# First batch of a Fourier and spatial-gating kernel: even transform summed as the fold goes, V by four products, W cast one piece ahead, four more W tiles ahead

## The chip, the cores and the metric

The kernel runs on one core of a Trainium2 chip. The metric is the device time of one execution in microseconds; where several executions are given, the median with the lowest and highest. TensorE is PE in the profile (its weight loads PEld), VectorE DVE, ScalarE ACT, GpSimd POOL, SyncE SP. All runs told here were in the fast state (mean granted clock, which is the TensorE clock in the profile as a share of full speed, 0.982 to 0.998 for the profiled ones), and all gave the right result. A DMA share is the mean busy share of the core's 16 DMA engines.

## The reference

```python
# x (8, 3072, 256), w_in (256, 1024), w_spatial W (3072, 3072), w_out (512, 256)
X = np.fft.fft(x, axis=1)
X = np.fft.fft(X, axis=2)
x = X.real.astype(np.float32)
h = np.maximum(x @ w_in, 0.0)
u, v = h[..., :512], h[..., 512:]
mu, var = mean(v), mean((v - mu) ** 2)           # over the last axis (cut)
v_n = (v - mu) / np.sqrt(var + 1e-06)
v_s = np.einsum('ts,bsd->btd', W, v_n) + b_spatial[None, :, None]
return ((u * v_s) @ w_out).astype(np.float32)
```

## The kernel before

Eight batches pass one after the other. For each, DVE folds x into even and odd sums, PE multiplies these with sine and cosine tables (the transform, four residues, even and odd halves in `eo`; a few rows are handled apart by a small product, the special columns or "specials", whose result is added when the transform leaves PSUM), then come the products with the folded `w_in` (V and U), then the big product with W, the spatial product. W must be transposed once, during the first batch, in 96 pieces of 128 x 768: load, cast to bf16, six transposes on PE, a copy out of PSUM into a W tile of four pieces, and a store of the finished tile for the later batches. There are 24 such tiles per batch (counted from 0 here), each used by four spatial groups of six products; after the fourth tile of every output chunk its output projection follows, so the first projection runs within tile 4. The tables, the first transform, the first V and the transposition of W all belong to the first 316 us.

A piece is cast when it is turned, so its transposes always wait for its own cast:

```python
def turn_w(wt, first=False):
    ...
    if first:
        nc.scalar.copy(out=wb, in_=src)              # cast on ACT, during the start
    else:
        nc.gpsimd.tensor_copy(out=wb, in_=src)       # cast on Pool, later
    load_w()
    for kk in range(GK):                             # six transposes on PE
        nc.tensor.transpose(pt[:, kk, :], wb[:, 128 * kk:128 * kk + 128], ident)
    ...                                              # copy to wt on DVE or ACT
    if r == 3:
        nc.scalar.dma_start(out=wtd[c][g], in_=wt)   # store of the finished tile
```

V is made for rows in mirrored pairs, with three products: their sum `pv`, and `pd`, twice the odd product. The mirrored row is `pv - pd`. It takes a copy on ACT and a subtraction on DVE:

```python
def v_pair(i, eo, pr):
    for kt in range(2):                              # pv = even + odd
        nc.tensor.matmul(pv, lhsT=eo[:, kt, sl], rhs=weo[:, kt, DH:], ...)
    nc.tensor.matmul(pd, lhsT=eo[:, 1, sl], rhs=wo2[:, DH:], ...)   # 2 x odd
    nc.scalar.activation(out=r[0], in_=pv, func=AF.Relu)
    nc.scalar.copy(out=m_, in_=pd)
def v_minus(...):
    nc.vector.tensor_tensor(out=r[1], in0=pv, in1=pd, op=ALU.subtract)
    ...                                              # statistics of r[0]
def v_relu(...):
    nc.scalar.activation(out=r[1], in_=r[1], func=AF.Relu)
# then: statistics of r[1] (DVE), root (ACT), reciprocal (DVE), norm (one half on ACT, one on DVE)
```

The start, in the order of issue: tables; three W pieces; per part of x an even fold, a piece, an odd fold, a piece; the special columns; then `dct_even` and `dct_odd` with a piece after each of the four residues; then V, in small steps among pieces. The pieces are capped at the four tiles that the spatial loop is ahead (`AHEAD = 4`).

## Time and profile before

| | before |
|---|---|
| time, 3 runs | 1420.38 us (1416.41 to 1420.64) |
| span of the profile, mean granted clock | 1418.0 us, 0.984 |
| first V product / sixth V pair normalised / twelfth | 69.05 / 98.76 / 133.67 |
| first output projection (tile 4) / second (tile 8) / fifth (tile 20) | 155.10 / 191.28 / 297.64 |

The span in 40 slices of 35.5 us each, a digit being the busy share in tenths (kernel before). Nearly all that PE loses lies in the first six slices, and its slow clock lies there too:

```profile
PE   0557989999999999999999999999999999999998
PEclk9968999999999999999999999999999999999999
DMA  7854888887444563345443563445434553444441
```

One V pair in the timeline of the kernel before (start, duration, engine, instruction, and in brackets the idle time of its engine before it with what ended that). DVE and ACT wait for each other in turn: ACT's norm for DVE's rs, DVE's statistics for ACT's Relu, which stands behind that norm. The round takes 94.53 - 90.31 = 4.22 us, though neither engine is full.

```profile
90.31 0.81 ACT L507 ACTIVATE v_t<-r,rs 128x512 bf16<-128x512 f32 x1 [1.62 <-DVE rs L505]
91.03 0.61 ACT L484 ACTIVATE r<-r 128x512 f32<-128x512 f32 x1
...
91.68 0.69 DVE L494 BATCH_NORM_STATS2 stt<-r 128x6 f32<-128x512 f32 x1 [1.01 <-ACT r L484]
...
94.53 0.81 ACT L507 ACTIVATE v_t<-r,rs 128x512 bf16<-128x512 f32 x1 [1.62 <-DVE rs L505]
```

### The profile page before, as it was taken

The page shows a single profiled execution, that of the slowest core. Times are in us where ns is not written, and L with a number is a line of the kernel's source. Part 1 is how long each engine was busy: PE and PEld are TensorE (multiplying, and loading weights), DVE is VectorE, ACT ScalarE, POOL GpSimd, SP SyncE. Part 2 cuts the span into 40 slices and gives each one's busy share as a digit, 9 for nine tenths or more (in the row PEclk, how much of TensorE's full clock was granted, in tenths as well). Part 3 has the DMA queues.
Part 4 walks back from the last instruction along what each step waited for, and adds up shares of the span by engine and source line. Part 5 has one row for each costly group of instructions (what it writes and reads, how often), then busy time and mean ns, then how long its engine had stood idle before and what let it go on. Part 6 is the DMA issues. An engine that isn't in the chain of part 4 may idle for free.

```text
span 1418.0 us, 18127 instructions
## 1 busy us (share of the span) xinstructions
PE 1327.9 (94%) x6955; PEld 651.9 (46%) x6955; DVE 860.4 (61%) x1715; ACT 515.9 (36%) x888; POOL 126.1 (9%) x167
## 2 busy tenths in 40 slices
PE   0557989999999999999999999999999999999998
PEld 0313545554444444444444444444444444444444
DVE  7465856676566755587376755587376755662323
ACT  4565235642245304441245314531345214541110
POOL 9112433440000000000000000000000000000000
PEclk9968999999999999999999999999999999999999
DMA  7854888887444563345443563445434553444441
GB/s 228 285 175 144 316 327 255 298 316 258 176 134 148 165 231 111 134 149 200 159 146 134 182 219 104 135 150 200 176 127 139 181 186 116 144 151 143 148 160 52
DMA packets 105255, 255.29 MB, mean 180 GB/s; under 512 B 17584, under 2 KB 64336, under 8 KB 105168
## 3 DMA queue, kind: packets, MB, share of 16 engines
q1 hardware_dynamic: 65840, 196.66, 41.9%
q10 hardware_dynamic: 29824, 44.05, 8.6%
q0 software_dynamic: 9504, 13.42, 3.0%
q8 instruction: 54, 0.88, 0.3%
q14 instruction: 33, 0.27, 0.1%
HBM read 210.80 MB, written 56.62 MB: 189 GB/s over the span
## 4 chain that ended last, share of the span: by engine, by line
PE 84%; DMA 3%; DVE 3%; ACT 1%; ACTq 0%; issue 0%; POOL 0%; SPq 0%; DVEq 0%; POOLq 0%
PE pw L543 66%; PE po L559 6%; PE pu L521 3%; PE pv L466 3%; PE pt L183 2%; PE pe L428 1%; PE pud L523 1%; PE pd L468 1%; DMA wr<-in_moe_w_spatial_dram 1%; DMA xt<-xr 1%; DVE tm L549 1%; DVE gt L550 1%; DVE xt L349 0%; DMA xt<-in_x_dram 0%; PE p L488 0%
## 5 line engine op out<-in xcount | busy, mean ns | idle before, releaser
L543 PE MATMUL pw<-wt,v_t 128*128 128x512 bf16 x4608 | 1054.5, 381 | 10.6 <-ACT v_t L507 10.5
L543 PEld LDWEIGHTS <-v_t 128*128 128x128 bf16 x4608 | 447.0, 98 | 530.2 <-issue 13.4
L563 ACT COPY ot<-po 128x512 f32<-128x512 f32 x96 | 56.3, 586 | 383.8 <-PE po L559 376.6
L549 DVE TENSOR_TENSOR tm<-pw,bbc 128x512 f32<-128x512 f32 x192 | 131.4, 684 | 95.0 <-PE pw L543 85.8
L507 ACT ACTIVATE v_t<-r,rs 128x512 bf16<-128x512 f32 x96 | 78.5, 817 | 108.7 <-DVE rs L505 102.3
L183 PE MATMUL pt<-ident,wb 128*128 128x128 bf16 x576 | 52.6, 233 | 52.1 <-ACT wb L177 45.7
L559 PE MATMUL po<-wob,gt 128*128 128x256 bf16 x768 | 99.7, 273 | 1.7 <-DVE gt L550 1.7
L526 ACT ACTIVATE up<-pu 128x512 bf16<-128x512 f32 x96 | 57.3, 597 | 110.8 <-PE pu L521 75.0
L179 POOL CAST wb<-wr 128x768 bf16<-128x768 f32 x87 | 75.8, 873 | 173.0 <-PE pt L183 136.7
L559 PEld LDWEIGHTS <-gt 128*128 128x128 bf16 x768 | 74.7, 98 | 29.3 <-DVE gt L550 2.2
L494 DVE BATCH_NORM_STATS2 stt<-r 128x6 f32<-128x512 f32 x96 | 65.3, 681 | 28.7 <-ACT r L484 28.2
L183 PEld LDWEIGHTS <-wb 128*128 128x128 bf16 x576 | 42.6, 104 | 77.9 <-ACT wb L177 48.4
L499 ACT ACTIVATE rs<-mv,epst 128x2 f32<-128x2 f32 x96 | 28.5, 297 | 120.1 <-DVE mv L495 112.9
L484 ACT ACTIVATE r<-r 128x512 f32<-128x512 f32 x96 | 60.2, 627 | 29.5 <-DVE r L478 27.6
L466 PE MATMUL pv<-weo,eo_t 128*128 128x512 bf16 x192 | 60.2, 397 | 10.8 <-ACT wt L188 3.4
L550 DVE SCALAR_TENSOR_TENSOR gt<-up,tm 128x512 bf16<-128x512 bf16 x96 | 67.5, 704 | 3.3
L550 DVE SCALAR_TENSOR_TENSOR gt<-um,tm 128x512 bf16<-128x512 bf16 x96 | 66.9, 696 | 3.3
L470 ACT ACTIVATE r<-pv 128x512 f32<-128x512 f32 x96 | 56.3, 586 | 33.0 <-PE pv L466 30.3
L188 ACT COPY wt<-pt 128x768 bf16<-128x768 bf16 x53 | 42.2, 796 | 65.5 <-PE pt L183 65.4
L479 DVE BATCH_NORM_STATS2 stt<-r 128x6 f32<-128x512 f32 x96 | 65.6, 684 | 0.0
L521 PE MATMUL pu<-eo_t,weo 128*128 128x512 bf16 x192 | 57.1, 379 | 0.0
L509 DVE TENSOR_SCALAR v_t<-r,mv,rs 128x512 bf16<-128x512 f32 x96 | 53.0, 553 | 0.0
(607 smaller groups left out, 971.6 us busy)
## 6 DMA issues: line engine op xcount, KB each, us to landing
wt<-wtd SPq DMA_DIRECT2D x168, 768.0 KB, 4.3
wr<-in_moe_w_spatial_dram SPq DMA_DIRECT2D x69, 384.0 KB, 4.5
out_dram<-ot ACTq DMA_DIRECT2D x88, 256.0 KB, 3.7
wtd<-wt ACTq DMA_DIRECT2D x24, 768.0 KB, 5.8
xr<-in_x_dram POOLq DMA_DIRECT2D x32, 384.0 KB, 11.3
xt<-in_x_dram SPq DMA_DIRECT2D x21, 512.0 KB, 4.2
xt<-xr SPq DMA_DIRECT2D x21, 512.0 KB, 6.5
wr<-in_moe_w_spatial_dram SPq DMA_DIRECT2D x23, 383.5 KB, 8.0
```

What stands on the lines that cost most here:

```text
L179: nc.gpsimd.tensor_copy(out=wb, in_=src)
L183: nc.tensor.transpose(pt[:, kk, :], wb[:, 128 * kk:128 * kk + 128], ident)
L466: nc.tensor.matmul(pv, lhsT=eo[:, kt, sl], rhs=weo[:, kt, DH:], start=(kt == 0), stop=(kt == 1))
L479: nc.vector.bn_stats(out=stt[:, 0, :], in_=r[0])
L484: nc.scalar.activation(out=r[1], in_=r[1], func=AF.Relu)
L494: nc.vector.bn_stats(out=stt[:, 1, :], in_=r[1])
L507: nc.scalar.activation(out=v[:, k, :], in_=r[0], func=AF.Identity, scale=rs[:, 0:1], bias=rs[:, 2:3])
L521: nc.tensor.matmul(ps, lhsT=weo[:, kt, wd], rhs=eo[:, kt, sl], start=(kt == 0), stop=(kt == 1))
L543: nc.tensor.matmul(pw, lhsT=v[:, k, 128 * dt:128 * dt + 128], rhs=wt[:, kk, :], start=(k == 0), stop=(k == KT - 1))
L549: nc.vector.tensor_tensor(out=tm, in0=pw, in1=bbc[:, TC * c:TC * c + TC], op=ALU.add)
L550: nc.vector.scalar_tensor_tensor(out=gt, in0=ut, scalar=0.0, in1=tm, op0=ALU.max, op1=ALU.mult)
L559: nc.tensor.matmul(po[:, i, :], lhsT=gts[dt][:, t0:t0 + 128], rhs=wob[:, dt, :], start=(dt == 0), stop=(dt == NDT - 1))
```

## The change

Its intent is to shorten the first batch in four places. The tables: less work for DVE, part of it moved to ACT. The even transform: each part's products are summed into PSUM banks as soon as the part is folded. V of the first batch: four products, with no copy and no subtraction, and for the first pairs in the banks of the spatial product (`psW`), which are still free; the root of a pair is put ahead of the next pair's work. W: a cast runs one piece ahead of its transposes, and four more tiles (`NX = 4`) are turned ahead, into the buffer that the second batch's V will need, by giving the first three tiles two pieces per spatial group.

```diff
+    def cast_w(first=False):
+        ...                                # the cast of turn_w, with a counter of its own
     def turn_w(wt, first=False):
+        while wstate["cast"] < i + 2 and wstate["cast"] < len(pieces):
+            cast_w(first)
+        wb = wbs.pop(i)
 ...
+    def dct_part(a, gx, banks):            # one part's even products, start=(a == 0)
+        ...
         def even(self, a):
             self.od, self.ev = fold_even(*self.xt)
+            if self.b == 0:
+                dct_part(a, (self.od, self.ev, None, None), self.pe0)
 ...
+    def v_both(i, eo, pr, first):          # first: banks of psW, else of psM
+        pv, pd, r = v_rows(i, eo, pr, first)
+        nc.tensor.matmul(pd, lhsT=eo[:, 0, sl], rhs=weo[:, 0, DH:], start=True, stop=False)
+        nc.tensor.matmul(pd, lhsT=eo[:, 1, sl], rhs=wo2[:, DH:], start=False, stop=True)
+        nc.scalar.activation(out=r[0], in_=pv, func=AF.Relu)
+        nc.scalar.activation(out=r[1], in_=pd, func=AF.Relu)
 ...
+        def v_first(self, i):
+            if i > 0:
+                v_root(i - 1, self.pr)
+            if i < NPAIR:
+                v_both(i, self.eo, self.pr, i <= EARLY)
+            if i > 0:
+                v_norm(i - 1, self.v, self.pr)
+            if i < NPAIR:
+                v_stat(i, self.pr, (0, 1))
 ...
+    NX = 4
+    def piece(first=False, at=-1):         # cap: AHEAD + NX tiles; the extra ones lie in wx
+        ...
         for dt in range(NDT):
             spatial(cur.v, wts[ti], pws[dt], g, dt)
+            for _ in range(PACE(ti)):      # 2 in tiles 0 to 2, then 1
+                piece(at=ti)
 ... (cut: tables moved to ACT, x reversal moved, later folds two tiles later)
```

## The prediction

> **What bounds the kernel now.** I read the busy times first, then the table of stages, then the engines' timelines in the first 300 us, then the chain of waits. TensorE is busy for 94% of the span, so only its idle time and its slow-clock time can be won. The table of stages (columns: stretch, length, busy time of PE, its weight loads, DVE, ACT, POOL, granted clock, DMA share, GB/s) shows where those are.
>
> ```profile
> PE 1327.9 (94%) x6955; PEld 651.9 (46%) x6955; DVE 860.4 (61%) x1715; ACT 515.9 (36%) x888; POOL 126.1 (9%) x167
> ...
> 0.00:57.00 57.00, 11.30 (x66) 6.47 (x67) 37.10 (x65) 28.12 (x35) 34.95 (x59) 1.00 0.77 240
> 57.00:69.00 12.00, 9.49 (x66) 5.06 (x64) 5.37 (x8) 6.41 (x7) 2.82 (x4) 1.00 0.97 305
> 69.00:100.00 31.00, 13.96 (x47) 4.56 (x48) 20.35 (x52) 20.43 (x37) 6.47 (x9) 0.61 0.62 213
> 100.00:134.00 34.00, 24.61 (x126) 11.45 (x124) 22.06 (x55) 19.43 (x38) 6.62 (x8) 0.85 0.43 120
> 134.00:163.00 29.00, 28.47 (x205) 16.43 (x206) 20.04 (x33) 8.03 (x12) 12.85 (x15) 0.94 0.75 254
> 163.00:193.00 30.00, 23.98 (x161) 12.84 (x160) 24.72 (x39) 6.14 (x9) 13.28 (x13) 0.94 0.93 339
> 193.00:292.00 99.00, 96.02 (x661) 53.33 (x660) 60.17 (x120) 53.13 (x87) 39.52 (x49) 0.98 0.82 277
> 292.00:316.00 24.00, 24.00 (x120) 11.63 (x119) 17.64 (x40) 12.17 (x22) 7.53 (x12) 1.00 1.02 374
> 316.00:474.00 158.00, 157.90 (x794) 76.14 (x793) 100.21 (x206) 56.67 (x101) 2.03 (x3) 1.00 0.53 180
> ```
>
> The spatial products of the second batch begin at 316.2 us; from there PE is full at full clock, and the change leaves that part as it is: 1418.0 - 316.2 = 1101.8 us stay. All that can move is the first 316 us. Within them the first spatial group completes only at 100, the third of the 24 W tiles starts at 134, and from 163 to 193 the DMA is the limit, although it was half idle from 69 to 134.
>
> Three waits make this. First lines: ACT turning W pieces in series. Then DVE waiting for the specials behind nine such pieces. Then the PE waiting for V:
>
> ```profile
> 32.67 0.83 ACT L177 CAST wb<-wr 128x768 bf16<-128x768 f32 x1
> 34.42 0.80 ACT L188 COPY wt<-pt 128x768 bf16<-128x768 bf16 x1 [0.92 <-PE pt L183]
> ...
> 56.83 0.22 DVE L409 COPY spb<-pb 128x64 f32<-128x64 f32 x1 [12.19 <-PE pb L407]
> ...
> 95.40 0.61 PE L543 MATMUL pw<-wt,v_t 128*128 128x512 bf16 x1 [3.62 <-ACT v_t L507]
> 99.62 0.61 PE L543 MATMUL pw<-wt,v_t 128*128 128x512 bf16 x1 [3.61 <-ACT v_t L507]
> ...
> 184.36 0.51 PE L183 MATMUL pt<-ident,wb 128*128 128x128 bf16 x6 [4.25 <-POOL wb L179]
> ```
>
> A piece costs 2.45 us on ACT (cast, wait for the transposes, copy), of which 0.92 is waiting. The folds on DVE had ended at 44.5, so ACT and not DVE sets 56.8. A V pair costs 4.22 us from 90 to 100. The last line is the shortage of W: Pool's cast was waiting for its load.
>
> **What the Trainium skill says.** "TensorE: Matmul & The Clock Gate", Part 1, has the PE at half clock after an idle window of about 3.4 us. The trace agrees: after the 3.6 us waits six spatial products take 2.13 us instead of 1.29. "PSUM — Partial Sum Buffer", Specifications, allows a VectorE instruction one tensor input from PSUM; this is why the old V pair copies one product to SBUF on ACT before DVE subtracts it (0.58 and 0.69 us in the trace). "ScalarE: Activation LUTs", What ACT_TABLE_LOAD costs, gives 1283 ns for a table load (the trace has 1.28) and 0.833 ns per element plus a fixed part, hence 1.45 us for a 1540-wide scaled copy, an estimate (the trace's 1540-wide Sin: 1.49 to 1.56). "DMA: Bandwidth & Descriptors", Issuing engines are not separate DMA queues, says DMAs of all engines share the same 16; the trace saturates at 340 to 390 GB/s (share about 1.0) whatever the queue mix.
>
> **The change, part by part.**
>
> *Tables.* The x reversal is issued before Pool's iotas, so the angle tables start 3.6 us later (their issue takes 3.58). In exchange y goes to ACT (3 x 1.45), the sign is put into the Sin, and the last scaling goes to ACT (2 x 1.45): DVE loses 3 x 1.1 + 3 x 0.27 + 1.5 = 5.6 us. ACT gets one more table load. I expect DVE free for the folds at 20 to 21 us instead of 24.25; but the identity of the transposes is still made by Pool at 20.9, so the first piece is copied at about 22.8 (was 32.8).
>
> *Pieces.* Casting one piece ahead removes the 0.92 us wait: 0.75 + 0.70 = 1.45 us per piece on ACT. From 22.8 on, ACT does: width Sines 0.7, third table 3.3, scalings 2.9 (29.7); wait for Pool's specials (6.9 us of Pool work after about 24.5: 31.7 with two Sines); a piece 1.45 and the width copies 3.8 (37.0); six pieces at 1.45 and two DMA issues at 0.4 (46.7). Specials and the last part sums on PE come at 45.4 to 47.
>
> *Even transform.* The banks are already summed, so four evictions (1.05 each) end at 51. The odd fold of the third part, now queued on DVE behind the specials (45.9 + 3.3 = 49.2), releases the odd products; evictions are shared by ACT and DVE, and the transforms are complete at about 56. Before: 69.0. Gain 13.
>
> *V.* Four products per pair in two banks of psW, so ACT does two Relus and no copy, DVE no subtraction. Per pair, DVE: 0.17 + 0.13 + 0.5 + 0.65 + 0.7 + 0.28 = 2.45; ACT: 0.3 + 0.5 + 0.55 + 0.75 = 2.1; with the 1.5 piece copies per pair about 2.9 each. The round of statistics, root, reciprocal, norm, statistics is also about 2.9. I take 3.1 against 4.22. First statistics at 56 + 4, table load 1.3, five more pairs 15.5, last norm 2: the first spatial group ends at about 78.5 to 79 (was 100.0).
>
> *Tiles 0 to 2.* Eight spatial groups at 1.29, 16 pieces at 0.336, five V pairs at 0.86, three U pairs at 0.7: about 21 us of PE, but V steps of 3.3 with U work in two of them need about 25, and the 12 small loads of the mirrored pieces plus two x reversals (3.1 MB, now both at this point) should hold Pool up for some 3 us. Third tile at about 106 (was 134.5).
>
> *Tiles 2 to 4*, still with pieces: 24 us of PE, and 8.5 MB or more of W, W-transposed and x, 23 to 25 us at 360 GB/s: ends at about 132 (was 156).
>
> *Tiles 5 to 8.* The buffers hold the pieces back at 52 of 96 until tile 9, so these tiles are pure spatial work: 16 x 1.29 + 2 x 0.87 + 0.65 = 23, ending at 155. Before, they ended at 192.8, with 16 pieces and the W waits (6 us and cold clock). This is where the four extra tiles pay: the W loads they need were moved into the idle DMA time before.
>
> *Tiles 9 to 19.* Same work as before: 44 groups, 44 pieces, the second batch's transform and V: 95.5 us of PE, about 99 before with its 3.6 us stall (an output DMA issue blocking ACT). I keep 100: 255. The second batch's folds are now two tiles closer to their transform, which may cost a little. *Tiles 20 to 23*: 24.2, second batch at 280 (was 316.2).
>
> Check by the other sum: TensorE needs 185.6 us for this loop (before) and 185.3 now (four pieces less, V pairs dearer). Before: 89.7 start + 185.6 + 41 lost. Now: 77 + 185 + 18 lost = 280. Extra TensorE work of the fourth product is only 12 x 0.22 = 2.6 us.
>
> Sum: 280 + 1101.8 = 1382 span, and the timed runs lie 2 us above the span of the profile: **1384 us**, 36 less, 2.6%.
>
> **The rivals.**
> 1. *The DMA takes back the gain.* Total W traffic is unchanged (96 pieces x 0.59 MB, read and written back), and it must now pass in 36 us less. For it: share 0.93 and a 6 us W wait at 163 to 193. Against it: 69 to 134 had share 0.43 to 0.62, and from 0 to 316 the mean is about 250 GB/s against a ceiling near 370. If tiles 0 to 4 are bound by loads (five buffers, many small loads, two reversals at once), 10 to 15 us go: 1395 to 1400.
> 2. *V or ACT stays at the old pace.* ACT inherits odd evictions, scalings, every second piece copy and the DMA issues, which can block it (one took 1.66 us). If a pair stays at 4 us, eleven pairs cost 9 us: about 1393. If the start slips too (specials on Pool, third odd fold queued late), about 1397.
> 3. *The clock and the next batch.* A fuller PE warms up earlier than I allow, and the rest of my 18 us lost shrinks to 8: 1374. Or the second batch's later folds stall its transform at tile 10: plus 2 to 5.
>
> **Range and chances.** Faster by over 2% needs less than 1392, that is 28 us won of the 36 I count. The parts worked out from engine times (start 13, V 8, piece-free tiles 13) are independent enough that one can fail by half. 8 in 10: 1369 to 1400. Faster 0.76, within 2% 0.23, slower 0.01.
>
> **What would show it.** Right: first V product near 56, first spatial group done near 79, second batch near 280, its own period unchanged at 157 to 158 us; no transposes for about 23 us between tiles 5 and 8; ACT pieces at 1.45 us without a 0.92 us wait. Wrong: Pool casts waiting on W loads for over 10 us between 80 and 135 (rival 1); V pairs at 4 us or more (rival 2); a longer period of the later batches, which I hold impossible; or new PE gaps where the third tile needs the last V.

## The result, and the profile after

The changed kernel took 1386.08 us (1385.82 to 1387.9, 4 runs) against 1419.23 us (1416.41 to 1420.64) of the kernel before on the same chip: faster, ratio 0.9772 with a 95% interval of 0.9753 to 0.979. A ratio here is the mean time of one kernel's fast runs over the mean of the other's fast runs of the same rounds, so not quite the ratio of the medians quoted. All outputs are right. The span of the profile is 1384.1 us, at a mean clock of 0.995.

The same slices after the change, now 34.6 us each. PE is fuller in the first four, the clock is below 0.9 in one slice only, and the DMA is busier in the third and fourth:

```profile
PE 1321.3 (95%) x6967; PEld 651.3 (47%) x6967; DVE 842.1 (61%) x1694; ACT 516.9 (37%) x890; POOL 128.6 (9%) x167
...
PE   1768999999999999999999999999999999999998
...
PEclk9989999999999999999999999999999999999999
DMA  7899699785444543356344653456344553444441
```

The pieces on ACT after the change: cast, copy, cast, with no 0.92 us wait between. The one shown takes 1.41 us from cast to cast; later ones before the transform take 1.42 to 1.63, or 1.94 with a store between.

```profile
36.91 0.81 ACT L189 CAST wb<-wr 128x768 bf16<-128x768 f32 x1
37.63 0.78 ACT L209 COPY wt<-pt 128x768 bf16<-128x768 bf16 x1
38.32 0.83 ACT L189 CAST wb<-wr 128x768 bf16<-128x768 f32 x1
```

DVE's wait for the specials is down from 12.19 to 5.75 us, and it ends at 45.0, not 56.8:

```profile
45.00 0.23 DVE L442 COPY spb<-pb 128x64 f32<-128x64 f32 x1 [5.75 <-PE pb L437]
```

The norms of three V pairs on ACT after the change are 3.06 and 2.68 us apart (4.22 before), and ACT no longer waits ahead of them:

```profile
60.71 0.81 ACT L588 ACTIVATE v_t<-r,rs 128x512 bf16<-128x512 f32 x1
...
63.77 0.81 ACT L588 ACTIVATE v_t<-r,rs 128x512 bf16<-128x512 f32 x1
...
66.45 0.81 ACT L588 ACTIVATE v_t<-r,rs 128x512 bf16<-128x512 f32 x1
```

Up to here all went as intended. The three largest gaps of PE from 77 us on, and the first piece-free stretch of the spatial product, show the other side. In tiles 0 to 4 PE waits for a cast on Pool, for ACT and for V; in tiles 5 to 8 it runs 48 products in a row, without transposes.

```profile
90.96 0.51 PE L204 MATMUL pt<-ident,wb 128*128 128x128 bf16 x6 [3.16 <-POOL wb L191]
...
103.69 0.38 PE L534 MATMUL pd<-weo,eo_t 128*128 128x512 bf16 x1 [3.41 <-ACT m__1148 L609]
...
113.80 0.39 PE L624 MATMUL pw<-wt,v_t 128*128 128x512 bf16 x1 [3.82 <-ACT v_t L588]
...
142.80 10.52 PE L624 MATMUL pw<-wx,v_t 128*128 128x512 bf16 x48
```

The second gap hangs on a store. ACT has the store of a finished W tile to issue, and the trace has ACT idle for 3.10 us in which that issue (0.33 us) falls last, its end put down to a load of W. Only then come the Relu of U and the copy that PE waits for.

```profile
102.18 0.33 ACTq L212 DMA_DIRECT2D wtd<-wx  x1
102.56 0.60 ACT L607 ACTIVATE up<-pu 128x512 bf16<-128x512 f32 x1 [3.10 <-DMA wr<-in_moe_w_spatial_dram]
```

By stages (start and end, length, busy time of PE, its weight loads, DVE, ACT and POOL, granted clock, DMA share, GB/s), first before, then after:

```profile
77.00:110.00 33.00, 17.13 (x68) 6.71 (x68) 22.28 (x57) 18.84 (x37) 2.49 (x4) 0.64 0.48 154
110.00:137.00 27.00, 17.67 (x85) 8.01 (x84) 15.77 (x40) 15.37 (x28) 4.96 (x6) 0.82 0.44 136
137.00:161.00 24.00, 24.00 (x180) 13.79 (x179) 17.46 (x25) 7.24 (x10) 11.01 (x13) 0.99 0.80 274
```

```profile
77.00:110.00 33.00, 26.06 (x176) 13.86 (x174) 16.75 (x47) 18.28 (x32) 13.03 (x16) 0.89 1.02 373
110.00:137.00 27.00, 21.99 (x178) 13.25 (x179) 18.38 (x31) 10.06 (x15) 16.06 (x17) 1.00 0.92 346
137.00:161.00 24.00, 23.69 (x117) 11.29 (x116) 14.92 (x29) 1.76 (x3) 0.64 (x1) 1.00 0.66 225
```

The idle DMA time of the kernel before (share 0.44 to 0.48 from 77 to 137 us) is now full (1.02 and 0.92), and the stage after it has slack.

So that kernels can be compared by stage, I cut the first 300 us at six marks of the trace: the first V product, the norm on ACT of the sixth and of the twelfth V pair, and the output projections in tiles 4, 8 and 20. The table gives the time between marks; it holds the kernels of the experiments too, since they are read against it.

| kernel | start to first V | to 6th V pair | to 12th V pair | to projection in tile 4 | to tile 8 | to tile 20 | sum |
|---|---|---|---|---|---|---|---|
| before | 69.05 | 29.7 | 34.9 | 21.4 | 36.2 | 106.4 | 297.6 |
| after | 55.03 | 20.3 | 37.6 | 23.0 | 23.3 | 104.9 | 264.0 |
| after, no extra tiles (E1) | 52.95 | 21.1 | 23.7 | 23.7 | 32.7 | 105.5 | 259.7 |
| after, V in three products (E2) | 54.70 | 33.7 | 42.6 | 23.9 | 23.3 | 104.6 | 282.7 |
| after, cast not ahead (E3) | 60.04 | 23.5 | 38.2 | 25.2 | 23.3 | 105.0 | 275.1 |
| before, with the V part (E8) | 68.02 | 19.6 | 25.7 | 20.1 | 34.1 | 108.0 | 275.4 |

From before to after, 33.6 us are won at tile 20: 14.0 at the start, 9.4 in the first six V pairs, minus 2.7 and minus 1.6 in the next two columns, 12.9 in tiles 5 to 8, 1.5 after. That looks like the prediction's bookkeeping. Whether those 12.9 us belong to the extra tiles is another question, and the experiments answer it differently.

### The profile page after: what moved, and what is told of

Its sections match the earlier page's. It is cut to its first block, busy times and chain, and to the rows that moved or that the text cites. A ratio compares the mean times of both kernels' runs of the same rounds, so it can differ in the third digit from the quotient of the medians.

```text
span 1384.1 us, 18120 instructions
## 1 busy us (share of the span) xinstructions
PE 1321.3 (95%) x6967; PEld 651.3 (47%) x6967; DVE 842.1 (61%) x1694; ACT 516.9 (37%) x890; POOL 128.6 (9%) x167
## 4 chain that ended last, share of the span: by engine, by line
PE 87%; DMA 5%; DVE 3%; ACT 2%; POOL 2%; issue 1%; ACTq 0%; SPq 0%; POOLq 0%; DVEq 0%
PE pw L624 68%; PE po L640 6%; DMA wr<-in_moe_w_spatial_dram 3%; PE pu L602 3%; PE pv L526 2%; PE pe L461 1%; PE pud L604 1%; PE pd L553 1%; PE pt L204 1%; DVE tm L630 1%; DMA xr<-in_x_dram 1%; DVE gt L631 1%; DMA wtd<-wx 1%; POOL xr L129 1%; POOL wb L191 0%
## 5 line engine op out<-in xcount | busy, mean ns | idle before, releaser
L624 PE MATMUL pw<-wt,v_t 128*128 128x512 bf16 x4512 | 1025.2, 380 | 7.8 <-ACT v_t L588 6.3
L204 PE MATMUL pt<-ident,wb 128*128 128x128 bf16 x576 | 48.9, 228 | 29.8 <-POOL ident L275 21.7
L567 ACT ACTIVATE r<-r 128x512 f32<-128x512 f32 x84 | 52.8, 628 | 28.2 <-DVE r L561 26.5
L554 ACT ACTIVATE r<-pv 128x512 f32<-128x512 f32 x84 | 49.3, 587 | 27.0 <-PE pv L526 26.7
L209 ACT COPY wt<-pt 128x768 bf16<-128x768 bf16 x44 | 35.1, 797 | 33.4 <-PE pt L204 33.3
```

The lines of the kernel that those rows point to most:

```text
L624: nc.tensor.matmul(pw, lhsT=v[:, k, 128 * dt:128 * dt + 128], rhs=wt[:, kk, :], start=(k == 0), stop=(k == KT - 1))
```

## The experiments

Theory after the result: the three parts each bring what the prediction gave them (start 13, V 8, extra tiles 13). Rivals: the extra tiles only move the wait for W from tiles 5 to 8 into tiles 0 to 4; V or the cast ahead carry more than their share. Each experiment undoes or adds one part. E1 to E4 ran together, and E5 to E8, and the last four, each of these on another chip; the kernel before in them took 1418.24, 1418.43 and 1418.86 us. "More than the change" means more than its 1386.08 us. It was run at another time. E10 shows that the same kernel can differ by 4 us. The mark of the first V product also scatters: in kernels that are alike up to there it came at 52.48 (E7), 55.03 (the change) and 56.52 us (E10).

**E1, no extra tiles.** The changed kernel, with the cap of pieces back at four tiles.

```diff
-    NX = 4
+    NX = 0
```

> The changed kernel without its four W tiles ahead (pieces then stop one tile earlier in the run-up and stay four tiles ahead). Milestones of the changed kernel: first V product 55.0 us, third W tile begun 108.8, tile 5 begun 136.8, tile 9 begun 160.7, second batch 282.6. Theory (the piece-free tiles 5 to 8 are where the lead pays): the start is unchanged to within 1 us, tiles 0 to 4 get 2 to 5 us shorter because fewer W loads and stores fall there, tiles 5 to 8 take 35 us or more instead of 23.9, and the run is 7 to 12 us longer than the changed kernel: 1393 to 1398. Rival (the lead only shifts the same DMA load, the gain is the earlier start alone): within 2 us of 1386.

Measured: 1384.06 us (1381.89 to 1387.42), ratio 0.9758 (0.974 to 0.9776). Taking the four tiles away costs nothing, where I had expected 7 to 12 us. In the table tiles 5 to 8 lengthen by 9.4 us, as a part that pays should show. But the stretch from the sixth to the twelfth V pair shortens by 13.9 us. (The profiled execution was the fastest of its four, so its sum in the table flatters it by some 2 us.) The same three stages of this kernel (columns as above): the DMA has room from 77 to 137 and is full from 137 to 161, the mirror image of the change.

```profile
77.00:110.00 33.00, 29.73 (x177) 14.93 (x176) 18.89 (x51) 18.55 (x35) 7.23 (x10) 0.92 0.86 300
110.00:137.00 27.00, 22.15 (x163) 12.66 (x162) 17.88 (x29) 6.24 (x9) 10.22 (x11) 1.00 0.72 242
137.00:161.00 24.00, 22.47 (x161) 12.52 (x159) 19.34 (x31) 7.90 (x12) 12.26 (x13) 1.00 1.01 378
```

The tile's store at this place goes out of ACT without a wait: what follows it waits only for its own product, 0.57 us, where the change had 3.10. It is not so for every store: later ones in this kernel still stand before 5.66 and 3.34 us of idle ACT (119.61 and 125.78 us).

```profile
90.50 0.60 ACT L607 ACTIVATE up<-pu 128x512 bf16<-128x512 f32 x1 [0.57 <-PE pu L615]
```

The shortage of W is still there later: at 131.72 us PE waits 3.05 us for a cast on Pool.

**E2, V in three products.** The changed kernel with the old arithmetic and the old order for the first batch: copy on ACT, subtraction on DVE, root after the next pair's work.

```diff
-            if i < NPAIR:
-                v_both(i, self.eo, self.pr, i <= EARLY)
+            if i < NPAIR:
+                banks = v_pair(i, self.eo, self.pr)     # ahead of the root
+                ...
+                v_minus(i, self.eo, self.pr, *banks)
             ...
-                v_stat(i, self.pr, (0, 1))
+                v_relu(i, self.eo, self.pr)
+                v_stat(i, self.pr)
```

> The changed kernel with the first batch's V by three products, a copy on ScalarE and a subtraction on VectorE, in the order of the kernel before and in the shared banks. Theory (the V round sets the time from 55 to 76.5 us): a pair takes about 4.2 us again instead of 2.65 to 3.2, the first spatial group ends 7 to 9 us later than 76.6, part of it stays to the end: 1391 to 1396. Rival (W pieces and DMA set the pace from the loop's start, so a slower V is hidden behind the stalls of tiles 0 to 2): the first group is late but the run is within 3 us of 1386.

Measured: 1404.3 us (1403.7 to 1405.22), 18 more than the change; more than both views had (1391 to 1396, or within 3 us of 1386). In the table, 13.4 us of it lie in the first six pairs and 5.0 in the next six. The norms on ACT now run at 5.19 us per pair ((88.35 - 62.41) / 5), where the kernel before had 4.46 over the same pairs and the change has 2.92. The waits of this kernel from 57 to 110 us (engine and line, what it waited for, total, times, longest) show the ring between ACT and DVE, and PE, too, waiting for ACT's piece copies that stand in the same queue:

```profile
ACT v_t L588 <- DVE rs L586: 14.5, 9, 2.0
DVE stt L574 <- ACT r L567: 7.4, 9, 1.0
PE pt L204 <- ACT wt L209: 7.2, 3, 2.5
```

and the granted clock falls to 0.59 from 57 to 77 us, where the change has 0.93 (its first line here, then E2's):

```profile
57.00:77.00 20.00, 12.51 (x97) 6.77 (x96) 17.23 (x51) 17.73 (x33) 13.84 (x18) 0.93 0.95 333
```

```profile
57.00:77.00 20.00, 10.57 (x56) 5.31 (x54) 13.29 (x32) 13.57 (x25) 5.76 (x7) 0.59 0.76 249
```

What follows: the old V is not a 4.22 us pair that can be taken over from the place where it ran undisturbed. With 1.5 W pieces per pair in the same two queues it takes 5.2 us, and PE goes cold beside it. This run undoes arithmetic, order and banks at once; it doesn't part the first two, and no later run does.

**E3, cast not ahead.** The changed kernel, each piece cast only when it is turned.

```diff
-        while wstate["cast"] < i + 2 and wstate["cast"] < len(pieces):
+        while wstate["cast"] < i + 1 and wstate["cast"] < len(pieces):
```

> The changed kernel with each W piece cast just before its transposes instead of one piece ahead. Theory (casting ahead is what shortened the start, 2.45 to 1.45 us a piece on ScalarE): eight pieces cost 0.92 us more each, the first V product moves from 55.0 to 60 to 63, and Pool's casts inside the loop leave gaps on TensorE where two pieces stand together: 1392 to 1398. Rival (VectorE's tables and folds set the start): first V product stays at 55 to 57, run within 2 us of 1386.

Measured: 1397.76 us (1396.18 to 1399.19), 12 more than the change, with the first V product at 60.04 (+5.0), the sixth pair 3.2 us later still, and some 3 us more up to tile 4. ACT has the old waits back:

```profile
43.05 0.80 ACT L209 COPY wt<-pt 128x768 bf16<-128x768 bf16 x1 [0.92 <-PE pt L204]
```

So one of the smallest edits of the whole change carries about a third of the gain, and not at the start alone.

**E4, even transform late.** The changed kernel with the even products of all parts after the last fold, as before.

```diff
             self.od, self.ev = fold_even(*self.xt)
-            if self.b == 0:
-                dct_part(a, (self.od, self.ev, None, None), self.pe0)
 ...
     for c in range(4):
+        cur.dct(c, dct_even)
         cur.dct(c, dct_odd)
```

> The changed kernel with the even transform done whole after the last fold, as before, instead of summed part by part. Theory: 18 products of 0.16 to 0.32 us (3 to 6 us) and four evictions move behind the specials; ScalarE's evictions were already the longer part, so the first V product comes 2 to 5 us later than 55.0 and the run is 1387 to 1391. Rival A (the sums as the fold goes are what won the 14 us of the start): 65 us or later, run 1396 or more. Rival B (it is all hidden behind the third odd fold, which VectorE ends at 49.5): first V product within 1 us of 55.0, run 1386.

Measured: 1388.79 us (1384.74 to 1391.38), 2.7 more than the change, but with a scatter that holds the change's own time; the first V product comes only 0.7 us later (55.74), less than that mark's own scatter, and the profiled run, the fastest of its four, was even 1.2 us shorter. The part named first in the title is worth 0 to 3 us. That is no more than these runs can resolve, and whether it is worth anything stays open.

**E5, reversal early.** The reversed copy of the second batch's x issued before the transform, not after the first V pairs.

```diff
         cur.odd(a)
+    xrs[1] = turn_x(1)
     for c in range(NCH):
 ...
-    xrs[1] = turn_x(1)
```

> The changed kernel with the reversal of the second batch's x issued right after the folds, as before, so that Pool and the DMA have one reversal instead of two at the start of the spatial loop (Pool spent 6.1 us there on eight issues, and the W casts at 79, 86 and 90 us waited for loads). Theory (tiles 0 to 2 lose their time to W loads that arrive late behind 3.1 MB of reversals): the gap of 3.2 us at 87.8 closes and the third tile begins 3 to 4 us earlier; run 1382 to 1384. Rival (bytes only move, the DMA is full from 57 to 110 anyway): within 1.5 us of 1386.

Measured: 1386.72 us (1385.09 to 1386.92), no difference, and the projection in tile 4 at 135.43 (135.88 in the change). The DMA is full in both stretches (share 0.99 from 45 to 57 us and 1.02 from 77 to 110 in the change, 1.03 and 1.04 here), so bytes moved from one to the other bring nothing.

**E6, store from Pool.** The store of a finished W tile issued by GpSimd, since ACT had stood 3.10 us before one.

```diff
-            nc.scalar.dma_start(out=wtd[c][g], in_=wt)
+            nc.gpsimd.dma_start(out=wtd[c][g], in_=wt)
```

> The changed kernel with the stores of the turned W tiles issued by Pool instead of ScalarE. In the changed kernel ScalarE stood 3.1, 1.5 and about 4 us in front of such an issue (the issue waits until an earlier transfer has landed), and the first of these left TensorE idle for 3.4 us at 100. Theory (ScalarE blocked by its DMA issues is part of what tiles 0 to 2 lose): those waits leave ScalarE, the third tile begins 3 to 5 us earlier, run 1381 to 1384. Rival: Pool is now blocked in their place, its casts come late, and the run is 1386 or more.

Measured: 1400.12 us (1398.37 to 1402.06), 14 more than the change. The store waits on Pool until its tile is ready, and the casts that the next pieces need stand behind it. From 57 to 145 us Pool stood 36.0 us in front of these stores; the profile puts 10.0 of them down to the last copy into the tile, and 10.3 to ACT's root, which in the case at 92.04 us runs right behind such a copy (ended at 91.75). PE waited 19.7 us for casts, where the change has 3.8:

```profile
PE pt L204 <- POOL wb L191: 19.7, 5, 7.4
...
POOL wtd L212 <- ACT rs L580: 10.3, 2, 6.0
...
POOL wtd L212 <- ACT wt L209: 5.3, 3, 2.6
POOL wtd L212 <- ACT wx L209: 4.7, 1, 4.7
```

The stores also go to another queue (in the profile 18.9 MB move from the hardware queue q10 to the software queue q0, and an issue takes 0.53 us instead of 0.33); what that alone costs is not parted from the waits. And the expectation had misread one of ACT's three waits: the one of about 4 us (3.63, before a store at 140.12) ended with DVE's copy into the tile (to 140.04), not with a transfer.

**E7, shared banks.** All four-product pairs in the psM banks that the pieces use as well.

```diff
-                v_both(i, self.eo, self.pr, i <= EARLY)
+                v_both(i, self.eo, self.pr, False)
```

> The changed kernel with the four products of a V pair in the shared PSUM banks, where the transposes also go, instead of the banks of the spatial products. Theory (the gain of V is in the arithmetic, two engine passes less per pair, not in the banks): a pair stays at 2.7 to 3.3 us, run within 3 us of 1386. Rival (the banks carry it): a pair takes 4 us, run 1392 or more.

Measured: 1388.22 us (1387.93 to 1391.33), 2.1 more than the change, with 3.00 us per pair over the first six, where the change has 2.92. The theory holds: the banks of the spatial product are worth about 2 us here, not clear of the scatter. As E2 used psM too, some 16 of its 18 us should be arithmetic and order (an estimate, since the two runs were made in different calls).

**E8, the V part alone.** The kernel before with nothing but the four-product V of the first batch, in its new order and the psW banks, with pieces between the first pairs, and the later pairs in the change's places in the spatial loop.

```diff
-    for u in range(EARLY):
-        for f in early[u]:
-            f()
-        if u % 4 == 0:
-            piece()
+    for i in range(7):
+        cur.v_first(i)
+        if i < 6:
+            piece()
```

> The kernel before with one part of the change alone: the first batch's V by four products in the banks of the spatial products, in the changed kernel's order. In the changed kernel, undoing this part cost 18 us. Theory (V production gates the first spatial group and then the third tile, whatever else is done): V still begins at 69, a pair takes about 3.1 instead of 4.2, the first group ends near 90 instead of 100, the third tile begins near 115 instead of 134; part of it is lost again to W loads: run 1403 to 1410. Rival (V only pays together with the earlier start and casting ahead): 1414 or more.

Measured: 1396.66 us (1395.49 to 1397.04), 22 less than the kernel before: more than I had expected, and two thirds of the whole gain. The table shows 10.1 us in the first six pairs (2.81 us per pair) and 9.2 in the next six, though the first V product is nearly as late as before (68.02). The idle DMA time fills as well, without any extra tile: share 0.63 from 77 to 110 us and 0.82 from 110 to 137, where the kernel before has 0.48 and 0.44.

**E9, V and the cast ahead.** The kernel of E8 with E3's edit the other way round: casting one piece ahead. Tables, even transform, reversal and the number of tiles ahead are the kernel before's.

```diff
-        wb = wbpool.tile([P, HW], BF16, name="wb", tag="wb")
-        ...                                # its cast
+        while wstate["cast"] < i + 2 and wstate["cast"] < len(pieces):
+            cast_w(first)
+        wb = wbs.pop(i)
```

> The kernel before with two parts of the change alone: the four-product V of the first batch (that alone gave 1396.66) and the casting one piece ahead. Tables, even transform, reversal and the number of tiles ahead stay as in the kernel before. Theory (V and cast together are nearly the whole change; undoing the cast in the changed kernel cost 12, undoing V 18): 1383 to 1388, first V product near 60 instead of 68. Rival (the moved tables and the even transform summed early carry a share that shows only in company): 1390 to 1395.

Measured: 1387.38 us (1386.57 to 1392.5, the profiled run being the slowest of the four), ratio 0.9787 (0.9769 to 0.9806). The change itself (E10) has 0.9796 (0.9782 to 0.981). Two parts of the change make as much gain as the whole. That does not say that the rest is worth nothing: it holds a gain and a loss, which E11 below parts. The first V product came at 60.91, near the 60 expected.

**E10 to E12, the number of tiles ahead once more.** E10 is the changed kernel itself as a control, E11 is E1's kernel, E12 has two extra tiles.

```diff
-    NX = 4
+    NX = 2      # E12 (E11: NX = 0, E10: no edit)
```

> The changed kernel itself once more, as a control for the two runs beside it: 1385 to 1388 by every theory.

> The changed kernel without the four extra tiles, once more with more rounds, since its first run lay 2 us below the change. Theory (the lead costs as much in tiles 0 to 4 as it returns in tiles 5 to 8, and its bursts of loads cost a little on top): 1382 to 1385, a difference of 1 to 4 us that holds. Rival (the 2 us were chance): 1385 to 1388, no difference.

> Two extra tiles in place of four. With four the DMA stands at a share of 1.02 at 77 to 110 us and 0.66 at 137 to 161; with none at 0.86 and 1.01. Theory (the cost is DMA saturation, and two levels it out): 1380 to 1383, under both. Rival (what is not lost at one place is lost at the other, since the same bytes must pass): between the two, 1383 to 1387.

| kernel | median (range) | ratio to before, 95% interval |
|---|---|---|
| E10, four extra (the change) | 1390.12 (1387.57 to 1390.9) | 0.9796, 0.9782 to 0.981 |
| E12, two extra | 1387.38 (1386.86 to 1387.86) | 0.9779, 0.9766 to 0.9792 |
| E11, none | 1384.69 (1383.58 to 1386.21) | 0.9762, 0.9748 to 0.9775 |

E11 lies below the change with intervals that do not touch, 0.34% of the kernel before's time (about 5 us); all four of its runs are faster than all four of E10's. E12 lies between, as the rival had it (its range of 1383 to 1387 was missed by 0.4 us). E9 has no extra tiles either, so it differs from E11 by the tables, the even transform, the reversal and the later folds: 1387.38 against 1384.69, with intervals that overlap. These parts bring the first V product 7.3 us earlier (60.91 to 53.65) and the time some 3 us, which is not clear of noise. The control missed its range: I gave 1385 to 1388 and it took 1390.12, so the same kernel moves by some 4 us. Differences of 2 or 3 us (E1, E4, E7) must be read with that. None of these reaches far, but the direction is the opposite of the intent: the version with no extra tiles beats both kernels.

What stays open: with two pieces per spatial group, tiles 0 to 2 have both more loads and stores in flight (DMA share 1.02) and more casts, transposes and copies in the engines' queues. E12's stretch from the sixth to the twelfth V pair took 37.3 us (73.12 to 110.43), as long as with four (37.6), although it takes in fewer extra bytes altogether. Whether the full DMA or the doubled pace stretches it is not separated by these runs. Nor is the arithmetic of V from its order, and no run takes the tables alone.

## Why the prediction was right or wrong

The time was right: 1384 predicted, 1386.08 measured, within the range. By its steps:

- *Start, first V near 56.* Right: 55.03. The ACT chain came within 1 us throughout (first piece copy 22.65 for 22.8, width copies done at 37.0 for 37.0, DVE's copy of the specials at 45.0 for 45.0, third odd fold done at 49.7 for 49.2). But the gain of 14 us there is not the even transform's: without it the mark comes 0.7 us later (E4), without the cast ahead 5.0 (E3). The rest of it is likely the tables', which no run takes alone.
- *V pair 3.1 us, first spatial group near 79.* Right: 2.92 us per pair over the first six, the group done at 76.6.
- *Third tile at 106.* Nearly: it began at 108.8, but its sixth product waited for the last V until 113.8. *Tile 5 at 132*: 136.75. This is the loss that rival 1 named for tiles 0 to 4. The sign of rival 1 was even met (Pool's casts waited 18.8 us for W loads from 80 to 135, over its 10), at a cost of about 5 us in these tiles (136.75 against 132) instead of its 10 to 15. So was the last sign of being wrong, a PE gap where the third tile needs the last V: 3.82 us.
- *Tiles 5 to 8 in 23 us, ending at 155.* The duration was right (23.9 us from 136.75, ending at 160.66).
- *The rest unchanged.* Right: second batch's spatial products from 282.6 (predicted 280), and 1101.5 us from there (1101.8 before).

**The step that failed** is the one in the sentence "This is where the four extra tiles pay: the W loads they need were moved into the idle DMA time before", with the 13 us credited for "piece-free tiles". The piece-free tiles do take 23 us, but without the extra tiles the whole is 2 to 5 us shorter (E1, E11). The idle DMA time that I read in the kernel before was idle because the first V was slow: with V alone made faster and no extra tile, its share from 110 to 137 us goes from 0.44 to 0.82 (E8). Once V and the start were shortened, the time from the first V to the projection in tile 4 was 68.5 us without the lead (E1: 121.45 - 52.95), and the extra pieces pushed it to 80.9. That gives back 12.4 us for 9.4 won. The profiles of E10 and E11 repeat it: 84.6 us with the lead against 66.6, and tiles 5 to 8 in 23.3 against 35.0. As I read it, I had counted the same idle time twice: once as time that V gives up, once as time in which loads are free. Whether the loads or the doubled pace of pieces takes the 12.4 us stays open.

**The terms that were mis-sized** made up for it, so that the total came within 2 us is partly luck. For V the prediction had 8 us; undone in the change it is worth 18 (E2), put alone into the kernel before 22 (E8). I had set 3.1 us against 4.22, the pace of the old pairs where no pieces ran among them; among pieces the old ring takes 5.19 (E2). The cast ahead was in the start term as about 1 us per piece on ACT; it is worth 12 (E3), of which some 7 come after the first V product, where I gave it nothing. The effects of undoing single parts, 18 + 12 + 2.7 - 2 = 31 us (E2, E3, E4, E1 against the change's 1386.08), come near the 33 us between the kernels, but they leave out the tables and come from several calls, so they don't show that the parts are independent; E9 reaches the change's time with V and the cast alone.

Rival 2 (V or ACT at the old pace) did not come about: no pair of the first six took over 3.5 us. Of rival 3, the clock did recover (0.93 from 57 to 77 us, 0.89 from 77 to 110), but the gaps in tiles 0 to 4 took its place.

Some of the prediction's readings and sums need putting right; none decides the result. Its "2.13 us instead of 1.29" sets the length of one group of six products against the distance from one group to the next; length against length it is 2.12 against 1.46, and the half clock shows better in the granted clock, 0.50 from 95.4 to 101.9 us. Its "340 to 390 GB/s" is not a ceiling that the trace shows: its own table has 305 GB/s at a share of 0.97, and 300 to 308 us has 401 at 1.03. The scaled copies on ACT took 1.58 and 1.56 us, near the 1563 ns of the formula in the Trainium skill, "ScalarE: Activation LUTs", What ACT_TABLE_LOAD costs, for an ACTIVATE with a pointer operand (280 + 0.833 N ns, N = 1540); but the second began 1.48 us after the first, so the estimate of 1.45 was nearly right as time in the queue. The PE work of tiles 0 to 2 adds up to 22.1 us, not 21, and the ACT chain to 46.5, not 46.7.

## What to carry to other kernels

Idle time of a shared resource, seen in a profile, belongs to the wait that causes it; when the same change removes that wait, do not also spend the idle time on something else, and test the prefetch by setting it to zero. Price a step that passes between two engines by the pace it has with the other work in those queues, not where it runs alone. Where a queue alternates "make" and "use" of the same piece, making the next one first is a few lines and may be a third of the gain.

## What the Trainium skill lacked or had wrong

- "DMA: Bandwidth & Descriptors", Issuing engines are not separate DMA queues, says that initiating DMAs on several engines only saves the sequencer's time to initiate, usually small. An issue took 0.33 us on ScalarE and 0.53 on GpSimd, against medians of 5.6 and 6.2 us from issue to landing (stores of W tiles from 57 to 150 us, the change and E6), which agrees. But the section lacks that an issue stands in its engine's order until its data is ready, and everything behind it with it: in the change ACT is idle for 3.63 us before the store at 140.12 us, which goes out when DVE's copy into the tile ends at 140.04. Moving the W tiles' stores from ScalarE to GpSimd, with the same 255.3 MB moved in all, cost 14 us (E6), and PE's waits for casts rose from 3.8 to 19.7 us.
- "ScalarE: Activation LUTs", What ACT_TABLE_LOAD costs, adds about 1380 ns of drain to the 1283 ns of the load, 2.66 us in all. Here the load for the first root started at 58.26, took 1.28 us, and the next ACTIVATE began at 59.56; the Relu before it had ended at 58.25. In the kernel before the load started at 74.12, 0.01 us after the copy ahead of it had ended, and the next ACTIVATE at 75.42. The switch cost about 1.3 us each time.
- None of the pages that I read has the pace of a two-engine round such as V's: 4.22 us alone, 5.19 among other work (E2), 2.92 with the copy and subtraction gone and the root first.
